# Chunk 1 of a fused attention and feed-forward kernel takes a seven-product gate pair, with its sums on GpSimd

## The chip, the cores and the metric

The kernel runs on one core of a Trainium2 chip. The metric is the device time of one execution in microseconds (us); the time before is 314.78 us, the median of three runs (314.7 to 315.67). The engines are TensorE (PE in the profile, with its weight loads as PEld), VectorE (DVE), ScalarE (ACT), GpSimd (POOL) and SyncE (SP). SP only issues DMAs here. Each engine takes its instructions in the order of the program, and waits at an instruction whose semaphores aren't there yet.

## The reference

Windowed attention over 8 batches of 576 positions and 8 heads of 64 (heads 0 to 3 with a window of 32, heads 4 to 7 with a window of 128 at a dilation of 4), whose output is the input `x` of a gated feed-forward block of 4608 tokens:

```python
scores = scale * np.matmul(q, k.transpose(0, 1, 3, 2))
scores = np.where(masks[None, :, :, :], scores, -1000000000.0)
attn = np.exp(scores - np.max(scores, axis=-1, keepdims=True))
attn = attn / (np.sum(attn, axis=-1, keepdims=True) + 1e-09)
out = np.matmul(attn, v)
x = out.transpose(0, 2, 1, 3).reshape(B * S, H * D)      # 4608 x 512
g = x @ w_gate                                            # 512 x 1536
gelu = 0.5 * g * (1.0 + erf(g * inv_sqrt2))
return (gelu * (x @ w_val) @ w_out)                       # 1536 x 512
```

## The kernel before

The 4608 tokens are nine chunks of 512. Each chunk c has a **gate stage** (x times the gate and value weights, twelve blocks of 128 columns of the inner width, giving `u_all`) and an **output stage** (`u_all` times the output weights). The attention of the next batch is done inside the stages of the chunk: its scores, sums and numerators stand between the output stage's matmuls, because chunk c needs batch c and a part of c - 1 only.

The order is written out by hand. `gate_words(c)` and `out_words(c)` give a string of words, and `run_program` (L1000) walks it and emits each word's instructions on their engines, in that order. A number n takes the next n matmuls of the stage's list. `g` and `u` are the gelu (ACT, L1028) and the product with the value half (DVE, L1033) of a block; `k` the sums of `u_all` for the output stage (DVE); `Kw@p` part p of the sums of the output weights `wo` number w, into `wx` (`weight_sums`, L754, on DVE); `h` the sums of the gate weights of a pair of blocks (`gate_sums`, L645, on GpSimd for pair 1); `Sn@..` the scores of head pair n (batch n // 4); `P`, `M`, `D`, `N`, `l`, `r`, `X` the steps of the softmax, where `X` (DVE, L614) writes x into `xT`.

Most products are done with seven products in place of eight on 2 x 2 blocks. In the output stages of chunks 1 to 8 this is done throughout (`seven`, L812), with the sums `wx` of the weights and `ux` of the data. In the gate stages it is done for some pairs of blocks (word `f`, `ffn1_seven`, L692): pair 1 (blocks 2 and 3) in chunks 2 and 3, two pairs in chunks 4 to 7, three in chunk 8, none in chunk 1. Such a pair is 28 matmuls of 256 columns, where the direct way takes 16 of 512 columns. Its products 1, 2 and 3 read `xT` itself. Products 6, 7, 5 and 4 read four sums of x, the tiles `x_sum` (word `x`, `x_sums`, L674): a chain of four elementwise operations, on GpSimd for the chunks in `free_pool` and on DVE otherwise. The products come in the order 1, 2, 6, 7, 5, 4, 3, spread between the direct blocks by `BLOCKS[c]`: a list of how many products follow each direct half block, and a string of what else is emitted there.

Loading a batch takes three steps. `F b` (`load_first`) has SP issue the loads of q and k of batch b as fp32 into the buffer `stage` (L210, L213, L224), and GpSimd cast them to fp16 into `s16` (L217, L229). `H b` (`load_rest`) has SP issue the transposes of `s16` (L272) and the loads of v (L241, L246, L250), which GpSimd casts too (L254). `R` in gate stage 2 is `H 3`, `F 4` and `H 4` together, and there the v of batch 3 is loaded by DMAs that GpSimd issues (L313, L321, L332). `stage` has three slots, which the loads use again and again. `F3`, the q and k of batch 3, stands at the head of gate stage 1.

Of the kernel before, what the change touches and what calls it, by code (L numbers as in the profile page):

```python
# [21 lines left out]
def kernel(  # L22
# [11 lines left out]
    B, H, S, D = q.shape  # L34
# [3 lines left out]
    NHP = H // 2  # L38
# [5 lines left out]
    NCH = NT // CH  # L44
    NNB = DFF // P
# [128 lines left out]
    def rows_in(src, r):  # L174

        return src.rearrange("h (p r) d -> p h (r d)", r=r)
# [450 lines left out]

    IN_PLACES = {c: {1: (1, 4), 2: (4, 1)} for c in range(4, 7)}
    IN_PLACES[2] = IN_PLACES[3] = {1: (1, 4)}
    IN_PLACES[7] = {1: (1, 4), 2: (2, 3)}  # L630
    IN_PLACES[8] = {1: (1, 2), 2: (6, 3), 3: (4, 5)}
    IN_SEVEN = {c: list(IN_PLACES[c]) for c in IN_PLACES}
    sums_at = {1: 0, 2: CH, 3: 2 * CH}
    free_pool = range(3, NCH)

    def sums_of(j, s):

# [282 lines left out]
    for h in range(0, HK, 2):  # L920
        for t, src, eng in ((0, q, nc.sync), (1, k, nc.scalar)):
            first = eng.dma_start(out=first_p[:, t, h : h + 2], in_=rows_in(src[0, h : h + 2], 6))
# [41 lines left out]
    def gate_banks(c, nb):  # L964

        if c == 0:
            return ((4, 5), (6, 7))[nb] if nb < 2 else ((0, 1), (2, 3))[nb % 2]
        if c in IN_SEVEN:
            if c == NCH - 1:
                return (3, 5) if nb == 10 else (0, 7)  # L970
            if c > 6 and nb > 1:
                return (3, 4) if nb == 11 else (5, 6) if nb % 2 else (0, 7)
            if nb in (1, 11):
                return (1, 4)
            return (4, 1) if nb == 9 and c < 4 else (0, 7)
        return ((0, 7), (1, 6) if c == 1 else (1, 4))[nb % 2]

    SEVEN = range(1, NCH)

    def gate_list(c):  # L980

        if c in firsts:
            first, seen = [], {}
            for word in firsts[c].split():
                nb, gi, kc = (int(x) for x in word)
                i = seen[nb, gi] = seen.get((nb, gi), 0) + 1
                first.append((nb, gi, (kc, i == 1, i == NKC)))
        else:
            first = [(nb, gi, part) for nb in range(2) for gi in range(2) for part in parts_of(range(NKC))]
        order = [(nb, gi) for nb in range(2, NNB) if nb // 2 not in IN_SEVEN.get(c, ()) for gi in range(2)]  # L990
        if c == 0:
            order = [(nb + n, gi) for nb in range(2, 10, 2) for gi in range(2) for n in range(2)] + order[16:]
        rest = [(nb, gi, part) for nb, gi in order for part in parts_of(range(NKC))]
        return [lambda m=m: ffn1_part(c, m[0], m[1], gate_banks(c, m[0])[m[1]], [m[2]]) for m in first + rest]
# [14 lines left out]
    def run_program(c, words, mms, banks):  # L1009
# [3 lines left out]
        for word in words.split():  # L1013
# [12 lines left out]
            elif kind == "g":  # L1026
                g = ffn.tile([P, CH], F16, tag="g")
                nc.scalar.activation(g, ps[:, gate_banks(c, args[0])[0], :], AF.Gelu)  # L1028
                tiles["g", args[0]] = g
            elif kind == "u":  # L1030
# [49 lines left out]
    def gate_words(c):  # L1080

        if c == 0:
            return (
# [4 lines left out]
            )  # L1088
        loads = {1: "F3", 2: "R", 3: "F5 H5", 4: "F6 H6", 5: "F7 H7"}.get(c, "")
        sums = [""] * NNB  # L1090
        if c in SEVEN:
            for j in range(NKP - 1):
                sums[2 * j + 1] += f" k{j}@0" + (f" k{j}@1@2 k{j}@2@2" if j % 2 else "")
        if c == min(SEVEN):
            for n, nb in enumerate((1, 2, 2, 4, 4, 4, 5, 6, 6, 8, 8, 8)):
                sums[nb] += f" K{n // 4}@{n % 4}"
        before = "" if c == NCH - 1 else f"q6@1@{c - 1}"
        last = f" u{NNB - 1} k5@0 k5@1 k5@2" if c > 6 else ""
        first = "7 G 1 g0 2 u0 4 g1 2 u1" if c < NCH - 1 else ""
        if c in IN_SEVEN:  # L1100
            words = seven_words(c)
            loads = f"{loads} x" if c == 2 else f"x z0 z1 {loads}" if c == 3 else f"x z1 {loads}" if c < 6 else "x z1 h3@0 h3@1 h3@2 h3@3" if c < 7 else "x" if c < NCH - 1 else loads
            return f"{before} {loads} {first} {words} 4 g{NNB - 1} {BLOCKS[c][2]} 4 {BLOCKS[c][3]}"
        blocks = [f"4 g{nb} 4 u{nb}{sums[nb]}" for nb in range(2, NNB - 1)]
        if c == 1:
            blocks[8] += f" S{2 * NHP}@12+S{2 * NHP + 1}@14"
        rest = " ".join(blocks)
        if c == 1:
            return f"{loads} 8 G 3 g0 1 u0 3 g1 1 u1{sums[1]} {rest} 4 g{NNB - 1} 4"
        return f"{before} {loads} {first}{sums[1]} {rest} 4 g{NNB - 1} 4{last}"  # L1110

    one = (
        [0, 1, 1, 0, 1, 1, 0, 1, 1, 1, 0, 0, 0, 0, 0],
        "||k0@0||k2@0||||k3@0|k3@1@2|U k3@2@2|U|U k1@0|k4@0 k1@1@2|k1@2@2",
    )
    two = (
        [0, 2, 2, 2, 2, 2, 2, 2, 0, 0, 0],
        "k0@0||||k3@0||k1@0|U|U k4@0 k1@1@2|U k2@0|k4@1@2",
    )
    both = ([0, 2, 2, 2, 2, 2, 2, 2, 0, 0, 0], "k0@0||||k3@0|||U|U k4@0|U k1@0 k2@0|k2@1@3")  # L1120
    BLOCKS = {c: (*two, "", "") for c in range(4, 7)}
    BLOCKS[3] = (*one, "", "")
    early = "h2@0||k0@0 h2@1||k2@0||h2@2||k3@0 h2@3|"
    BLOCKS[2] = (one[0], one[1].replace("||k0@0||k2@0||||k3@0|", early).replace("U k1@0", "U k1@0 S12@12+S13@15"), "", "")
    three = ([0, 3, 3, 3, 3, 3, 3, 3, 0, 0, 0], "||||k0@0|||k1@0|U k4@0|U|U k2@0 k3@0")
# [4 lines left out]
    def seven_words(c):  # L1130

        places = IN_PLACES[c]
        order = (1, 2, 6, 7, 5, 4, 3)
        turns = [(j, product) for j in places for product in order]
        if c > 6:
            turns = [(j, product) for product in order for j in places]
        if len(places) > 2:
            turns = [("_abc".index(w[0]), int(w[1])) for w in in_turn.split()]
        groups = [f"f{j}@{product}@{places[j][order.index(product) % 2]}" for j, product in turns]
        pairs = list(places)  # L1140
        direct = [nb for nb in range(2 if c < NCH - 1 else 0, NNB - 1) if nb // 2 not in pairs]
        slots, after = BLOCKS[c][0], BLOCKS[c][1].split("|")
        words = [groups.pop(0) for _ in range(slots[0])] + [after[0]]
        for n, nb in enumerate(direct):
            for part in range(2):
                words.append(f"4 {'gu'[part]}{nb}")
                for _ in range(slots[2 * n + part + 1]):
                    words.append(groups.pop(0))
                words.append(after[2 * n + part + 1])
        assert not groups  # L1150
        return " ".join(words)

    def out_words(c):

        if c == 0:
            return (
                "h1@0 h1@1 h1@2 h1@3 V1 F2 S6@4+S7@6 1 E P6 11 P7 1 M6 S4@4+S5@6 M7 1 P4 6 P5 M4 2 D6@40+D7@60 l6 l7 M5 r6 r7 6 w2@0 4 w1@0 4 "
                "w0@0 H2 N6@50+N7@20 D4@52+D5@22 X6 l5 X7 l4 r4 r5 10 N4@20+N5@40 X4 X5 2 e3@0"
            )
        if c > 6:  # L1160
            return "12 q0@1 x8 12 q1@1 12 q2@1 12 q3@0 12 q4@0 12 q5@0 12 q6@1" if c < NCH - 1 else "L"
        i, j, k, l = (NHP * (c + 1) + n for n in range(NHP))
        v0 = " v0" if 2 < c < 6 else ""
        some = "k5@1@2 k5@2@2" if len(IN_SEVEN.get(c, ())) < 2 else "k5@1@2@3 k1@2@2 k3@2@2 k5@2@2"
        after = f"S{l + 1}@12+S{l + 2}@15" if 1 < c < 6 else ""
        return (
            f"E P{i} P{j} 1 u11 k5@0 11 q0@0 M{i} M{j}{v0} {some} 12 q1@1 8 "
            f"S{k}@1+S{l}@4 D{i}@11+D{j}@41 P{k} P{l} 8 q2@0 M{k} M{l} 8 l{i} l{j} r{i} r{j} q3@0 "
            f"12 N{i}@10+N{j}@40 D{k}@12+D{l}@42 q4@0 X{i} l{l} X{j} l{k} r{l} r{k} 12 q5@0 {6 if c < 3 else 4} "
            f"N{k}@13+N{l}@43 {after} X{l} X{k} {6 if c < 3 else 8}"  # L1170
        )
# [10 lines left out]
    def run_chunk(c):  # L1182

        banks = out_banks(c)
        run_program(c, gate_words(c), gate_list(c), banks)
        run_program(c, out_words(c), out_list(c, banks), banks)
# [31 lines left out]
```

## Time and profile before

One profiled execution took 314.36 us, with a span of 312.6 us from the first to the last instruction. It is split here by the starts of the stages, as the chain of the work that ended last has them. A row holds the length of the stage and the busy time of each engine, in us.

| stage | from, us | length | PE | DVE | ACT | POOL |
|---|---|---|---|---|---|---|
| output 0 | 41.90 | 13.36 | 13.36 | 8.33 | 8.60 | 8.42 |
| output 1 | 76.55 | 11.98 | 11.98 | 10.59 | 9.48 | 3.37 |
| gate 2 | 88.53 | 20.89 | 20.89 | 17.53 | 11.31 | 10.52 |
| output 3 | 142.56 | 12.26 | 12.26 | 10.91 | 9.42 | 4.61 |
| gate 4 | 154.82 | 20.68 | 20.68 | 16.79 | 14.36 | 12.74 |
| output 4 | 175.50 | 11.76 | 11.66 | 10.37 | 8.75 | 2.10 |

The busy time of PE is read as the time in which any matmul is under way; where it equals the length of a stage, PE never waited there. The mean duration of a matmul in the profile (379 ns for 512 columns) is longer than its share of a stream, because consecutive matmuls overlap.

### The profile page before, as it was taken

To read this page: it belongs to the slowest core of one execution; us is meant where nothing else is said; L and a number is where in the kernel's file an instruction comes from. 1 tells how busy PE (TensorE), PEld (TensorE's weight loads), DVE (VectorE), ACT (ScalarE), POOL (GpSimd) and SP (SyncE) were. 2 spreads that over 40 slices of the span, in tenths; PEclk is the share of its full clock that TensorE was granted. 3 is DMA by queue.
4 is the path that set the end of the run, shared out by engine and by line. 5 is a ranking of instruction groups with operands and counts; after the bars stand their busy time and mean duration, and the time that the engine had idled before them with its cause. 6 is when DMAs were issued, how large, how long until landed. Compare 5 with 4: busy or idle time off the path is not lost.

```text
span 312.6 us, 8913 instructions
## 1 busy us (share of the span) xinstructions
PE 306.2 (98%) x3645; PEld 198.9 (64%) x3645; DVE 238.4 (76%) x425; ACT 189.0 (60%) x320; POOL 126.2 (40%) x174
## 2 busy tenths in 40 slices
PE   7999999999999999999999999999999999999995
PEld 4754555445855486557756685668566856687674
DVE  6773657698897896589868986998698859936972
ACT  2673376534774586547767677777677765427640
POOL 8884774321358073627074327412750073000000
PEclk9999999999999999999999999999999999999999
DMA  8999997897799999789788978995100220021004
GB/s 187 188 200 206 204 202 137 219 235 180 174 282 167 192 192 192 197 197 234 154 238 191 211 183 220 229 182 157 67 3 1 69 69 2 0 94 42 2 0 135
DMA packets 110792, 47.17 MB, mean 151 GB/s; under 512 B 83616, under 2 KB 110240, under 8 KB 110752
## 3 DMA queue, kind: packets, MB, share of 16 engines
q1 hardware_dynamic: 97248, 38.29, 54.9%
q0 software_dynamic: 12944, 7.67, 17.9%
q10 hardware_dynamic: 560, 0.66, 0.8%
q8 instruction: 28, 0.46, 0.6%
q14 instruction: 12, 0.10, 0.1%
HBM read 37.75 MB, written 9.44 MB: 151 GB/s over the span
## 4 chain that ended last, share of the span: by engine, by line
PE 92%; DVE 2%; DMA 2%; ACT 1%; issue 1%; POOL 1%
PE ps L623 44%; PE ps L812 23%; PE ps L692 13%; PE ps L458 7%; PE ps L737 3%; DMA xT<-in_k_dram 2%; PE ps L378 1%; DVE u_all L1033 1%; ACT P L488 1%; DVE xT L614 0%; DVE ux L778 0%; DVE u_all L733 0%; PE ps L447 0%; POOL xT L182 0%; DVE ux L773 0%
## 5 line engine op out<-in xcount | busy, mean ns | idle before, releaser
L623 PE MATMUL ps<-xT,wv 128*128 128x512 f16 x328 | 85.6, 379 | 0.0
L623 PE MATMUL ps<-xT,wg 128*128 128x512 f16 x328 | 84.7, 379 | 0.1
L1028 ACT ACTIVATE g<-ps 128x512 f16<-128x512 f32 x82 | 48.9, 597 | 57.9 <-PE ps L623 57.8
L1033 DVE SCALAR_TENSOR_TENSOR u_all<-g,ps 128x512 f16<-128x512 f16 x82 | 56.0, 684 | 34.8 <-PE ps L623 18.4
L623 PEld LDWEIGHTS <-wg 128*128 128x128 f16 x328 | 31.8, 98 | 33.2 <-issue 0.2
L623 PEld LDWEIGHTS <-wv 128*128 128x128 f16 x328 | 32.1, 98 | 31.7 <-issue 0.8
L812 PEld LDWEIGHTS <-u_all 128*128 128x128 f16 x390 | 36.3, 98 | 7.0 <-issue 0.3
L812 PE MATMUL ps<-wx,ux 128*128 128x256 f16 x288 | 35.2, 272 | 0.1
L812 PE MATMUL ps<-wo,u_all 128*128 128x256 f16 (+1 forms) x294 | 35.2, 271 | 0.0
L217 POOL CAST s<-stage 128x640 f16<-128x640 f32 x24 | 18.8, 812 | 38.5 <-DMA stage<-in_q_dram 24.0
L614 DVE TENSOR_TENSOR xT<-ps,rb 128x576 f16<-128x576 f32 x32 | 29.0, 936 | 4.5 <-PE ps L458 2.9
L488 ACT ACTIVATE P<-ps 128x832 f16<-128x832 f32 (+1 forms) x32 | 25.3, 835 | 11.4 <-PE ps L458 11.3
L812 PEld LDWEIGHTS <-ux 128*128 128x128 f16 x288 | 28.1, 98 | 4.0 <-issue 0.3
L254 POOL CAST v<-stage 128x1152 f16<-128x1152 f32 x11 | 13.1, 1188 | 39.6 <-DMA stage<-in_v_dram 31.3
L692 PEld LDWEIGHTS <-xT 128*128 128x128 f16 x208 | 20.2, 98 | 8.4
L674 POOL TENSOR_TENSOR x_sum<-xT 128x512 f16<-128x512 f16 x12 | 14.0, 1170 | 27.9 <-DVE xT L614 26.5
L733 DVE SCALAR_TENSOR_TENSOR u_all<-g,quarter 128x256 f16<-128x256 f16 x47 | 23.2, 497 | 2.7 <-ACT g L724 2.7
L773 DVE TENSOR_TENSOR ux<-u_all 128x512 f16<-128x512 f16 x48 | 23.4, 493 | 0.8
L585 ACT ACTIVATE lg<-ps 128x576 f32<-128x576 f32 x30 | 18.8, 655 | 7.3 <-PE ps L458 4.3
L724 ACT ACTIVATE g<-quarter 128x256 f16<-128x256 f32 x47 | 19.2, 415 | 4.0 <-DVE quarter L716 3.9
L692 PE MATMUL ps<-x_sum,xT 128*128 128x256 f16 x156 | 21.4, 273 | 0.0
L229 POOL CAST s<-stage 128x512 f16<-128x512 f32 x24 | 17.3, 752 | 6.1 <-DMA stage<-in_q_dram 4.3
(120 smaller groups left out, 432.7 us busy)
## 6 DMA issues: line engine op xcount, KB each, us to landing
out_dram<-part SPq DMA_DIRECT2D x30, 256.0 KB, 3.2
stage<-in_v_dram SPq DMA_DIRECT2D x28, 144.0 KB, 3.6
stage<-in_q_dram SPq DMA_DIRECT2D x24, 128.0 KB, 3.7
stage<-in_k_dram SPq DMA_DIRECT2D x24, 128.0 KB, 2.9
stage<-in_q_dram SPq DMA_DIRECT2D x6, 512.0 KB, 4.6
stage<-in_k_dram SPq DMA_DIRECT2D x6, 512.0 KB, 5.5
stage<-in_v_dram SPq DMA_DIRECT2D x20, 128.0 KB, 2.9
wo<-in_moe_w_out_dram POOLq DMA_DIRECT2D x3, 512.0 KB, 16.6
```

Source lines behind the costliest of these rows:

```text
L217: nc.gpsimd.tensor_copy(s16[:, 1280 * t + 640 * g : 1280 * t + 640 * g + 640].rearrange("p (k c) -> p k c", k=5), st_of(i).rearrange("p (k ...
L458: nc.tensor.matmul(o[cols], lhs[rows], rhs[rows], start=st, stop=end, skip_group_check=True)
L488: nc.scalar.activation(pt[:, 0 : src.shape[1]], src, AF.Exp, bias=0.0, scale=scale)
L614: nc.vector.tensor_tensor(dst, num, rb, ALU.mult)
L623: nc.tensor.matmul(ps[:, bank, :], w[:, kc, ns], xT[kc][:, tok], start=first, stop=end)
L692: nc.tensor.matmul(ps[:, bank, 2 * P * m : 2 * P * m + 2 * P], left[:, k], right[:, k], start=first and m == 0 and k == 0, stop=k == 1, sk ...
L724: nc.scalar.activation(g, t[:, 0 : 2 * P], AF.Gelu)
L733: nc.vector.scalar_tensor_tensor(dst, g, by, t[:, 2 * P : 4 * P], ALU.mult, ALU.mult)
L773: nc.vector.tensor_tensor(ux[:, j, 0:2], k0, u_all[:, 2 * j : 2 * j + 2, hi], ALU.subtract)
L812: lambda o=o, s=s[:, P * p : P * p + P], t=t[:, c0:c1], st=st, end=end: nc.tensor.matmul(o, s, t, start=st, stop=end, skip_group_check=True)
L1028: nc.scalar.activation(g, ps[:, gate_banks(c, args[0])[0], :], AF.Gelu)
L1033: nc.vector.scalar_tensor_tensor(u_all[:, nb, :], tiles.pop(("g", nb)), -USCALE if c in SEVEN and nb % 2 else USCALE, val, ALU.mult, ALU.mult)
```

## The change

Chunk 1 joins the chunks with a seven-product gate pair: pair 1, blocks 2 and 3, in banks 1 and 4. Its x sums go to GpSimd (`free_pool` gets 1), and the word `x` is put behind `F3` at the head of gate stage 1. The twelve parts of the output weights' sums (`K`), all in gate stage 1 before, are split: the eight of `wo` 0 and 1 go to output stage 0, the four of `wo` 2 stay. The scores of batch 2 in gate stage 1 move a bank on and a little forward. The first scores of batches 4 and 5 (`S16`, `S17` and `S20`, `S21`) go from the ends of output stages 2 and 3 into gate stages 3 and 4. The gate weights' sums for pair 1 (`h1`) stay where they were, at the head of output stage 0.

```diff
     IN_PLACES[2] = IN_PLACES[3] = {1: (1, 4)}
+    IN_PLACES[1] = {1: (1, 4)}
...
-    free_pool = range(3, NCH)
+    free_pool = (1, *range(3, NCH))
...
             if nb in (1, 11):
-                return (1, 4)
+                return (1, 6 if c + nb == 2 else 4)
             return (4, 1) if nb == 9 and c < 4 else (0, 7)
-        return ((0, 7), (1, 6) if c == 1 else (1, 4))[nb % 2]
+        return ((0, 7), (1, 4))[nb % 2]
...
-        if c == min(SEVEN):
-            for n, nb in enumerate((1, 2, 2, 4, 4, 4, 5, 6, 6, 8, 8, 8)):
-                sums[nb] += f" K{n // 4}@{n % 4}"
-        before = "" if c == NCH - 1 else f"q6@1@{c - 1}"
+        before = "" if c in (1, NCH - 1) else f"q6@1@{c - 1}"
         last = f" u{NNB - 1} k5@0 k5@1 k5@2" if c > 6 else ""
         first = "7 G 1 g0 2 u0 4 g1 2 u1" if c < NCH - 1 else ""
+        if c == 1:
+            first, loads = "8 G 3 g0 1 u0 3 g1 1 u1", f"{loads} x"
         if c in IN_SEVEN:
             words = seven_words(c)
-            loads = f"{loads} x" if c == 2 else f"x z0 z1 {loads}" if c == 3 else ...
+            loads = loads if c == 1 else f"{loads} x" if c == 2 else f"x z0 z1 {loads}" if c == 3 else ...
             return f"{before} {loads} {first} {words} 4 g{NNB - 1} {BLOCKS[c][2]} 4 {BLOCKS[c][3]}"
         blocks = [f"4 g{nb} 4 u{nb}{sums[nb]}" for nb in range(2, NNB - 1)]
-        if c == 1:
-            blocks[8] += f" S{2 * NHP}@12+S{2 * NHP + 1}@14"
         rest = " ".join(blocks)
-        if c == 1:
-            return f"{loads} 8 G 3 g0 1 u0 3 g1 1 u1{sums[1]} {rest} 4 g{NNB - 1} 4"
...
-    BLOCKS[3] = (*one, "", "")
+    BLOCKS[3] = (one[0], one[1].replace("U k1@0", "U k1@0 S16@12+S17@15"), "", "")
+    BLOCKS[4] = (two[0], two[1].replace("k4@0", "k4@0 S20@12+S21@15"), "", "")
+    BLOCKS[1] = (
+        one[0],
+        one[1].replace("||k0@0||k2@0||||k3@0|", "K2@0||k0@0|K2@1|k2@0|K2@2|||k3@0 K2@3|").replace("k1@2@2", "k1@2@2 S8@12+S9@15"),
+        "",
+        "",
+    )
...
         if c == 0:
             return (
-                "... l6 l7 M5 r6 r7 6 w2@0 4 w1@0 4 "
-                "w0@0 H2 N6@50+N7@20 D4@52+D5@22 X6 l5 X7 l4 r4 r5 10 N4@20+N5@40 X4 X5 2 e3@0"
+                "... l6 l7 M5 K0@0 K0@1 r6 r7 6 w2@0 4 w1@0 4 "
+                "w0@0 H2 N6@50+N7@20 D4@52+D5@22 X6 l5 X7 K0@2 K0@3 l4 r4 r5 10 N4@20+N5@40 X4 X5 K1@0 K1@1 K1@2 K1@3 2 e3@0"
             )
...
-        after = f"S{l + 1}@12+S{l + 2}@15" if 1 < c < 6 else ""
+        after = f"S{l + 1}@12+S{l + 2}@15" if 3 < c < 6 else ""
```

The diff gives `x` one letter; what it does to an engine's queue is seen in the order of its instructions. On GpSimd, from the cast of the v of batch 1 in output stage 0 on, the program before has this (the first four L217 and L229 rows are batch 2, `v_102` is the v of batch 2, the second L217 and L229 rows are `F3`, and `v_100` is the v of batch 3 from `R`):

```order
L254 CAST v_101<-stage 128x1152
L217 CAST s_107<-stage 128x640 x4
L229 CAST s_107<-stage 128x2x4x64 x4
L297 COPY q_104<-q_104 128x8x16
L254 CAST v_102<-stage 128x1152 x2
L217 CAST s_107<-stage 128x640 x4
L229 CAST s_107<-stage 128x2x4x64 x4
L313 DMA v_100<-in_v_dram 64x2x256
```

and the changed program this, from the same v of batch 2 on:

```order
L254 CAST v_102<-stage 128x1152 x2
L217 CAST s_107<-stage 128x640 x4
L229 CAST s_107<-stage 128x2x4x64 x4
L675 TENSOR_TENSOR x_sum<-xT 128x512
L675 TENSOR_TENSOR x_sum<-xT,x_sum 128x512
L675 TENSOR_TENSOR x_sum<-xT 128x512
L675 TENSOR_TENSOR x_sum<-xT,x_sum 128x512
L313 DMA v_100<-in_v_dram 64x2x256
```

The four x sums of chunk 1 stand behind the eight casts of batch 3's q and k, and ahead of the DMAs that load batch 3's v. The order on SP is the same in both programs.

On TensorE, in gate stage 1 after the second half of block 5, the program before goes on with the next direct block:

```order
L623 LDWEIGHTS wv_94
L623 MATMUL ps<-xT,wv_94 128x512
L623 LDWEIGHTS wg_90
L623 MATMUL ps<-xT,wg_90 128x512 [waits Activation_49]
L623 LDWEIGHTS wg_90
```

The changed program has product 6 of the pair there, the third of its seven products (what an instruction waits for stands in brackets):

```order
L623 LDWEIGHTS wv_94
L623 MATMUL ps<-xT,wv_94 128x512
L693 LDWEIGHTS xT [waits Activation_49]
L693 MATMUL ps<-x_sum,xT 128x256 [waits Pool_49]
L693 LDWEIGHTS xT
L693 MATMUL ps<-x_sum,xT 128x256
```

The first matmul of product 6 waits for GpSimd, and all later matmuls of the kernel are behind it on TensorE. (Where block 5's second half stands in the chunk differs between the two, since blocks 2 and 3 are no longer direct.)

On DVE, at the end of output stage 0, the program before stores three output tiles, writes the x of batch 1 and starts on the blocks of gate stage 1:

```order
L493 TENSOR_TENSOR P_994<-P_994,two_p 128x832
L750 TENSOR_SCALAR osb<-ps 128x512 x3
L614 TENSOR_TENSOR xT<-ps,rb 128x576 x4
L1033 SCALAR_TENSOR_TENSOR u_all<-g,ps 128x512 x2
L773 TENSOR_TENSOR ux<-u_all 128x512
```

The changed program has eight of the weight sums among them:

```order
L493 TENSOR_TENSOR P_994<-P_994,two_p 128x832
L761 TENSOR_TENSOR wx_110<-wo_96 128x512
L763 TENSOR_TENSOR wx_110<-wx_110,wo_96 128x512
L751 TENSOR_SCALAR osb<-ps 128x512 x3
L614 TENSOR_TENSOR xT<-ps,rb 128x576 x2
L765 TENSOR_TENSOR wx_110<-wo_96 128x512
L767 SCALAR_TENSOR_TENSOR wx_110<-wx_110,wo_96 128x512
L614 TENSOR_TENSOR xT<-ps,rb 128x576 x2
L761 TENSOR_TENSOR wx_111<-wo_97 128x512
L763 TENSOR_TENSOR wx_111<-wx_111,wo_97 128x512
L765 TENSOR_TENSOR wx_111<-wo_97 128x512
L767 SCALAR_TENSOR_TENSOR wx_111<-wx_111,wo_97 128x512
```

Two sums stand ahead of the stores, two between the pairs of x writes, and four behind the last x write.

More of the change, by code (lines that the diff above doesn't have):

```diff
@@ L1093, in gate_words @@
                 sums[2 * j + 1] += f" k{j}@0" + (f" k{j}@1@2 k{j}@2@2" if j % 2 else "")
-        if c == min(SEVEN):
-            for n, nb in enumerate((1, 2, 2, 4, 4, 4, 5, 6, 6, 8, 8, 8)):
-                sums[nb] += f" K{n // 4}@{n % 4}"
-        before = "" if c == NCH - 1 else f"q6@1@{c - 1}"
+        before = "" if c in (1, NCH - 1) else f"q6@1@{c - 1}"
         last = f" u{NNB - 1} k5@0 k5@1 k5@2" if c > 6 else ""
         first = "7 G 1 g0 2 u0 4 g1 2 u1" if c < NCH - 1 else ""
+        if c == 1:
+            first, loads = "8 G 3 g0 1 u0 3 g1 1 u1", f"{loads} x"
         if c in IN_SEVEN:
             words = seven_words(c)
-            loads = f"{loads} x" if c == 2 else f"x z0 z1 {loads}" if c == 3 else f"x z1 {loads}" if c < 6 else "x z1 h3@0 h3@1 h3@2 h3@3" if c < 7 else "x" if c < NCH - 1 else loads
+            loads = loads if c == 1 else f"{loads} x" if c == 2 else f"x z0 z1 {loads}" if c == 3 else f"x z1 {loads}" if c < 6 else "x z1 h3@0 h3@1 h3@2 h3@3" if c < 7 else "x" if c < NCH - 1 else loads
             return f"{before} {loads} {first} {words} 4 g{NNB - 1} {BLOCKS[c][2]} 4 {BLOCKS[c][3]}"
         blocks = [f"4 g{nb} 4 u{nb}{sums[nb]}" for nb in range(2, NNB - 1)]
-        if c == 1:
-            blocks[8] += f" S{2 * NHP}@12+S{2 * NHP + 1}@14"
         rest = " ".join(blocks)
-        if c == 1:
-            return f"{loads} 8 G 3 g0 1 u0 3 g1 1 u1{sums[1]} {rest} 4 g{NNB - 1} 4"
         return f"{before} {loads} {first}{sums[1]} {rest} 4 g{NNB - 1} 4{last}"
@@ L1156, in out_words @@
             return (
-                "h1@0 h1@1 h1@2 h1@3 V1 F2 S6@4+S7@6 1 E P6 11 P7 1 M6 S4@4+S5@6 M7 1 P4 6 P5 M4 2 D6@40+D7@60 l6 l7 M5 r6 r7 6 w2@0 4 w1@0 4 "
-                "w0@0 H2 N6@50+N7@20 D4@52+D5@22 X6 l5 X7 l4 r4 r5 10 N4@20+N5@40 X4 X5 2 e3@0"
+                "h1@0 h1@1 h1@2 h1@3 V1 F2 S6@4+S7@6 1 E P6 11 P7 1 M6 S4@4+S5@6 M7 1 P4 6 P5 M4 2 D6@40+D7@60 l6 l7 M5 K0@0 K0@1 r6 r7 6 w2@0 4 w1@0 4 "
+                "w0@0 H2 N6@50+N7@20 D4@52+D5@22 X6 l5 X7 K0@2 K0@3 l4 r4 r5 10 N4@20+N5@40 X4 X5 K1@0 K1@1 K1@2 K1@3 2 e3@0"
             )
```

## The prediction, made before the changed kernel ran

> **What bounds the kernel now.** I read the page's first part, then the busy time by stage, then the chain of work that ended last.
>
> ```profile
> span 312.6 us, 8913 instructions
> PE 306.2 (98%) x3645; PEld 198.9 (64%) x3645; DVE 238.4 (76%) x425; ACT 189.0 (60%) x320; POOL 126.2 (40%) x174
> ```
>
> TensorE lacks 6.4 us of the span. The view by stage (length, then the busy time of each engine with its instructions) shows that none of it lies in gate stages 1 and 3:
>
> ```profile
> 55.26:76.55 21.29, 21.29 (x134) 9.80 (x133) 17.39 (x34) 9.26 (x15) 5.63 (x8) 1.00 0.90 211
> 109.42:122.23 12.81, 12.47 (x282) 10.45 (x280) 12.13 (x17) 9.48 (x14) 6.56 (x9) 1.00 1.13 193
> 122.23:142.56 20.33, 20.33 (x111) 10.61 (x109) 13.58 (x27) 11.32 (x21) 9.39 (x10) 1.00 0.79 202
> ```
>
> The first row is gate stage 1, the second output stage 2, which lacks 0.34 us, the third gate stage 3. So time is TensorE's work plus whatever makes TensorE wait, and a wait of TensorE goes into the total one for one. The chain in order of time (start, length, what) gives the work's shape in gate stage 1 and, as a pattern with one seven-product pair, gate stage 3:
>
> ```profile
> 55.26 18.99 PE ps L623 x88
> 74.25 0.47 PE ps L458 x36
> ...
> 76.55 3.49 PE ps L812 x32
> ...
> 122.23 4.32 PE ps L623 x20
> 126.55 0.44 PE ps L692 x4
> 126.98 0.86 PE ps L623 x4
> 127.85 0.44 PE ps L692 x4
> 128.28 1.73 PE ps L623 x8
> 130.01 0.44 PE ps L692 x4
> ```
>
> A direct matmul (L623) takes 4.32 / 20 = 0.216 us of the stream, one of a seven-product pair (L692) 0.44 / 4 = 0.11 us.
>
> **The change, part by part.** *The pair itself.* Sixteen direct matmuls go (16 x 0.216 = 3.46 us), 28 short ones come (28 x 0.109 = 3.05 us): 0.41 us less. Stage against stage it is 0.49: gate stage 3 has what the new gate stage 1 will have but for the scores of batch 2, so 20.33 + 0.47 = 20.80 against 21.29. I take **-0.49 us**.
>
> *The x sums.* Product 6 is the third of the pair, and the first that reads one of them. In gate stage 3 it starts at 130.01 - 122.23 = 7.78 us. Both stages begin with 16 direct matmuls and keep the same slots, so in the new gate stage 1 TensorE comes to it at 55.26 + 7.78 = 63.04 us. When is its sum there? GpSimd runs in order, and the change puts the four sums behind the eight casts of batch 3's q and k. The timeline of GpSimd before shows when these run (start, length; in brackets the idle time ahead and what ended it):
>
> ```profile
> 61.48 2.79 POOL L229 CAST s<-stage 128x512 f16<-128x512 f32 x4 [1.44 <-DMA stage<-in_q_dram]
> 67.62 0.30 POOL L297 COPY q<-q 128x128 f16<-128x128 f16 x1 [3.35 <-DMA q<-s]
> 74.86 1.15 POOL L254 CAST v<-stage 128x1152 f16<-128x1152 f32 x1 [6.95 <-DMA stage<-in_v_dram]
> 78.85 1.22 POOL L254 CAST v<-stage 128x1152 f16<-128x1152 f32 x1 [2.83 <-DMA stage<-in_v_dram]
> 83.22 1.80 POOL L217 CAST s<-stage 128x640 f16<-128x640 f32 x2 [3.16 <-DMA stage<-in_q_dram]
> 88.18 1.39 POOL L217 CAST s<-stage 128x640 f16<-128x640 f32 x2 [3.16 <-DMA stage<-in_k_dram]
> 89.51 1.55 POOL L229 CAST s<-stage 128x512 f16<-128x512 f32 x2
> 92.12 1.18 POOL L229 CAST s<-stage 128x512 f16<-128x512 f32 x2 [1.06 <-DMA stage<-in_k_dram]
> ...
> 123.05 1.15 POOL L674 TENSOR_TENSOR x_sum<-xT 128x512 f16<-128x512 f16 x1 [4.22 <-DVE xT L614]
> 124.28 1.16 POOL L674 TENSOR_TENSOR x_sum<-xT,x_sum 128x512 f16<-128x512 f16 x1
> ```
>
> The first row is batch 2; the casts from 83.22 on are batch 3's, and the last ends at 92.12 + 1.18 = 93.30 us, more than a stage behind the words that emit it. GpSimd isn't busy; it waits for transfers, and their issue is late. The queue of SP:
>
> ```profile
> 76.43 2.38 SPq L210 DMA_DIRECT2D stage<-in_q_dram  x4
> 84.93 0.60 SPq L224 DMA_DIRECT2D stage<-in_q_dram  x1
> 85.63 1.42 SPq L224 DMA_DIRECT2D stage<-in_k_dram  x1
> 87.17 3.38 SPq L835 DMA_DIRECT2D out_dram<-part  x4
> ```
>
> SP comes to batch 3's loads at 76.43 us, after the stores of chunk 0, the transposes of batch 2 and its v, and the order on SP is unchanged. None of those waits for a matmul of gate stage 1, so a stopped TensorE neither hastens nor delays them. Product 6 reads the second sum made. From the start of the first sum to the end of the second it is 124.28 + 1.16 - 123.05 = 2.39 us, so by these rows the sum is there at 93.30 + 2.4 = 95.7 us. It may come sooner: the last load took 6.4 us from its issue to its landing, where the six of its kind took
>
> ```profile
> DMA to landing us min/median/max: 4.0/4.9/6.4
> ```
>
> and the stores of output stage 1, which went out right behind it, won't be there. But the casts ahead of the last two (1.39 + 1.55 us from 88.18) hold GpSimd until 91.1, so at best the last pair starts there, 1.0 us earlier: 94.6 us. I take the middle, 95.1. TensorE then waits 95.1 - 63.04 = **+32.1 us** (31.6 to 32.7). Behind product 6 nothing waits longer: the third sum is wanted one direct half block on and comes one operation (1.16 us) later. Queued behind the waiting matmul is the rest of the kernel. Queued behind the sums on GpSimd are the DMAs of batch 3's v: 93.24 us before, about 98 after, for numerators that move out by the whole stall.
>
> *The restart.* TensorE sits idle for 32 us, and no row shows it doing so inside this kernel. The nearest is the start of the program, where it comes from idle as well:
>
> ```profile
> 1.53 3.84 PE L905 MATMUL ps<-ones 128*32 128x32 f16 x73 [1.53 <-DVE ones L67]
> L905 PE MATMUL ps<-ones 128*128 128x512 f16 x4 | 1.9, 627 | 0.0
> L623 PE MATMUL ps<-xT,wv 128*128 128x512 f16 x328 | 85.6, 379 | 0.0
> ```
>
> The first four matmuls of 512 columns take 1.9 us together, 0.47 each against 0.216 in the stream, and 627 ns each against 379. From its first matmul at 1.53 to the end of those it is some 3.7 us at about half rate, which loses half of that. I take **+1.8 us** for the restart, between 0 (the granted clock is 1.00 in every slice of the page, the first too) and 3.6 (twice as long).
>
> The Trainium skill, "TensorE: Matmul & The Clock Gate", section "What's actually happening", says that TensorE's clock falls to half after an idle window of about 3.4 us, and comes back after about 3.4 us of sustained work. By that the restart would cost half of 3.4, an estimate of 1.7 us, in place of the 1.8 above; and the stall would cost nothing more than itself if the rule did not hold. The slow first matmuls agree with it, the granted clock of this profile does not show it.
>
> *The weight sums.* Twelve parts go from a gate stage in which DVE is busy 17.39 of 21.29 us. Two groups stand for them: three of the four parts take about 0.41 us, the fourth 0.68.
>
> ```profile
> L766 DVE SCALAR_TENSOR_TENSOR wx<-wx,wo 128x512 f16<-128x512 f16 x3 | 2.0, 681 | 0.0
> L760 DVE TENSOR_TENSOR wx<-wo 128x512 f16<-128x512 f16 x3 | 1.2, 412 | 0.0
> 49.37 0.69 DVE L750 TENSOR_SCALAR osb<-ps 128x512 f32<-128x512 f32 x1 [1.14 <-PE ps L737]
> 54.83 1.42 DVE L614 TENSOR_TENSOR xT<-ps,rb 128x576 f16<-128x576 f32 x2 [0.96 <-PE ps L458]
> 58.30 0.69 DVE L1033 SCALAR_TENSOR_TENSOR u_all<-g,ps 128x512 f16<-128x512 f16 x1 [2.04 <-ACT g L1028]
> ```
>
> The last three rows are DVE's in output stage 0, with its idle gaps. The two parts ahead of the stores (0.83 us) fit in the gap of 1.14; the next two (1.09) in 0.96, late by 0.13, while x is wanted by the fifth matmul of gate stage 1, at 55.26 + 0.86, and is there at 55.6 instead of 55.5; the last four (1.92) in 2.04. So **0**. If the cover failed, x would be late by 0.1 to 0.9 us, and that much shorter the stall, whose end GpSimd sets: again 0. The four left in gate stage 1 run in the stall.
>
> *The moved scores.* Their matmuls are the same, 0.47 us out of output stages 2 and 3 and into gate stages 3 and 4: 0 for TensorE. What can go is the 0.34 us in output stage 2; by the timeline it isn't at those scores but ahead of them, so I take **-0.2**, between -0.34 and 0. With 32 us of idle TensorE the later loads also have more time; since TensorE lacks nothing in the gate stages after, that gives nothing back.
>
> **The sum.** -0.49 + 32.1 + 1.8 - 0.2 = +33.2 us. The profiled execution took 314.36 us (1.76 beyond its span), so 347.6; the median is 0.42 above it, so **348.0 us**.
>
> **The rivals.** (1) *The sums are early enough.* If batch 3's casts were done by 60 us, the sums would be there before 63.04, and what is left is -0.49 - 0.2: 314.1, no change by measure. The point that decides is the end of the casts, 93.30 against 60.6. For it speaks only that GpSimd idles much of the stage (5.63 us busy of 21.29); against it stands that these idle times end with transfers issued after 76.43. Chance 0.04. (2) *No restart cost*: TensorE goes on at full rate, 346.2 us. The granted clock of 1.00 speaks for it, the first matmuls against. Chance 0.22. (3) *A second wait* follows, because batch 3's v or batch 4 comes too late behind the sums: some 3 us and more, 351 or above. Against it: SP's next work, the stores of output stage 1, moves out with TensorE, while GpSimd loses under 5 us of 32. Chance 0.06. The forecast, a stall of about 32 us with a slow restart, has 0.68.
>
> **How the numbers follow.** Lowest: 31.6 - 0.49 - 0.34 + 0 gives 314.36 + 30.8 = 345.1. Highest: 32.7 - 0.49 + 0 + 3.6 with the 0.42 to the median gives 350.6. This range holds the forecast and rival 2. About 0.3% (0.9 us) is what a measurement can tell from no change: slower takes the forecast, rivals 2 and 3 (0.96); rival 1 falls within it, with 0.01 for a gain beyond it (0.03 and 0.01).
>
> **What would show it.** TensorE busy until about 63 us, then idle until about 95, its wait put down to GpSimd's `x_sum`; the sums on GpSimd right behind the cast that ends at 92 to 93; the first matmuls after it longer than 379 ns; gate stage 1 some 53 to 55 us long, all later stages as before within 0.5 us. Wrong would be: sums that run before 83 us, an idle time under 30 us, or a later stage that has grown.

## The result, and the profile after

The changed kernel takes 345.63 us, the median of six runs (344.9 to 347.08), against 315.0 us for the kernel before, timed on the same chip (six runs, 314.7 to 316.08). The ratio is 1.0983, with a 95% interval of 1.0962 to 1.1003: 30.6 us longer, and slower. The prediction was 348.0 us, with a range of 345.1 to 350.6. The profiled execution took 344.90 us, the shortest of the six and 0.2 us below that range.

The first lines of the page after, and from its view in 40 slices (8.6 us each) the rows of TensorE's busy time and granted clock:

```profile
span 343.2 us, 8950 instructions
PE 307.9 (90%) x3657; PEld 200.9 (59%) x3657; DVE 237.9 (69%) x430; ACT 191.1 (56%) x326; POOL 128.5 (37%) x178
...
PE   8999999300199999999999999999999999999996
...
PEclk9999999855589999999999999999999999999999
```

TensorE's busy time grew by 1.7 us only, its idle time by 28.9, and a little more than all of that lies in one hole, slices 8 to 11. The clock is granted at half rate in most of the hole, and the slice behind it isn't at full rate either. The busy time by stage after, with gate stage 1 cut at the hole (columns as before: length, PE, PEld, DVE, ACT, POOL, then the granted clock, the DMA share and GB/s):

```profile
55.03:62.87 7.84, 7.84 (x40) 3.81 (x39) 6.83 (x14) 4.75 (x7) 3.48 (x6) 1.00 0.90 262
62.87:92.77 29.90, 0.00 (x0) 0.00 (x0) 1.67 (x4) 0.00 (x0) 10.82 (x16) 0.54 0.76 172
92.77:107.74 14.97, 14.97 (x106) 7.75 (x106) 9.02 (x19) 6.62 (x14) 8.67 (x12) 0.88 0.49 39
107.74:119.55 11.81, 11.81 (x246) 9.90 (x244) 9.86 (x16) 9.47 (x14) 0.00 (x0) 1.00 0.15 48
119.55:140.44 20.89, 20.89 (x146) 10.94 (x145) 17.45 (x39) 11.30 (x21) 4.97 (x7) 1.00 0.98 202
140.44:152.29 11.85, 11.85 (x246) 9.93 (x244) 10.42 (x17) 9.47 (x14) 1.94 (x4) 1.00 0.86 165
```

For 29.90 us neither TensorE nor ACT does anything, and DVE 1.67 us of work. Output stage 1 and gate stage 2 (the fourth and fifth row) are as long as before within 0.2 us, and output stage 2 has lost its wait. What ended the hole is seen on GpSimd; its timeline after, in the same columns as before:

```profile
81.62 1.39 POOL L217 CAST s<-stage 128x640 f16<-128x640 f32 x2 [2.68 <-DMA stage<-in_q_dram]
84.60 1.39 POOL L217 CAST s<-stage 128x640 f16<-128x640 f32 x2 [1.59 <-DMA stage<-in_k_dram]
87.83 1.18 POOL L229 CAST s<-stage 128x512 f16<-128x512 f32 x2 [1.85 <-DMA stage<-in_q_dram]
89.20 1.18 POOL L229 CAST s<-stage 128x512 f16<-128x512 f32 x2 [0.20 <-DMA stage<-in_k_dram]
90.33 1.15 POOL L675 TENSOR_TENSOR x_sum<-xT 128x512 f16<-128x512 f16 x1
91.57 1.15 POOL L675 TENSOR_TENSOR x_sum<-xT,x_sum 128x512 f16<-128x512 f16 x1
```

The sums run right behind batch 3's casts, as fast as in the other chunks. The second one ends at 92.72, and the matmuls of TensorE after it are

```profile
92.77 1.01 PE L693 MATMUL ps<-x_sum,xT 128*128 128x256 f16 x4 [29.90 <-POOL x_sum L675]
93.58 1.91 PE L623 MATMUL ps<-xT,wg 128*128 128x512 f16 x4
95.28 1.06 PE L693 MATMUL ps<-x_sum,xT 128*128 128x256 f16 x4
96.14 1.09 PE L623 MATMUL ps<-xT,wv 128*128 128x512 f16 x4
97.06 1.03 PE L623 MATMUL ps<-xT,wg 128*128 128x512 f16 x4
```

with the four direct matmuls at 93.58 taking 1.91 us, where four of the same shape take 1.03 from 97.06 on. Two questions are left: is it the sums' place in GpSimd's queue, and is the slow restart due to the idling?

### The profile page after: what moved, and what is told of

Its sections match the earlier page's. It is cut to its first block, busy times and chain, and to the rows that moved or that the text cites. A ratio compares the mean times of both kernels' runs of the same rounds, so it can differ in the third digit from the quotient of the medians.

```text
span 343.2 us, 8950 instructions
## 1 busy us (share of the span) xinstructions
PE 307.9 (90%) x3657; PEld 200.9 (59%) x3657; DVE 237.9 (69%) x430; ACT 191.1 (56%) x326; POOL 128.5 (37%) x178
## 4 chain that ended last, share of the span: by engine, by line
PE 87%; SPq 4%; DMA 4%; POOL 1%; ACT 1%; DVE 1%; issue 1%; POOLq 0%
PE ps L623 40%; PE ps L813 22%; PE ps L693 13%; PE ps L458 6%; PE ps L738 3%; DMA q<-s 2%; DMA stage<-in_k_dram 2%; SPq L210 1%; PE ps L906 1%; PE ps L378 1%; SPq L241 1%; SPq L213 1%; SPq L246 1%; POOL x_sum L675 1%; PE ps L375 1%
## 5 line engine op out<-in xcount | busy, mean ns | idle before, releaser
L1034 DVE SCALAR_TENSOR_TENSOR u_all<-g,ps 128x512 f16<-128x512 f16 x80 | 54.7, 685 | 65.0 <-PE ps L623 51.0
L623 PE MATMUL ps<-xT,wg 128*128 128x512 f16 x320 | 83.5, 382 | 0.2
L623 PE MATMUL ps<-xT,wv 128*128 128x512 f16 x320 | 83.7, 379 | 0.0
L1029 ACT ACTIVATE g<-ps 128x512 f16<-128x512 f32 x80 | 47.7, 597 | 57.3 <-PE ps L623 55.4
L693 PE MATMUL ps<-x_sum,xT 128*128 128x256 f16 x168 | 24.1, 279 | 29.9 <-POOL x_sum L675 29.9
L623 PEld LDWEIGHTS <-wv 128*128 128x128 f16 x320 | 31.4, 98 | 30.2 <-issue 1.1
L693 PEld LDWEIGHTS <-xT 128*128 128x128 f16 x224 | 22.2, 99 | 40.0 <-issue 30.7
L707 ACT COPY vdiag<-ps 128x512 f32<-128x512 f32 x22 | 12.8, 582 | 37.0 <-POOL x_sum L675 31.2
L675 POOL TENSOR_TENSOR x_sum<-xT 128x512 f16<-128x512 f16 x14 | 16.4, 1169 | 40.2 <-DVE xT L614 38.8
L217 POOL CAST s<-stage 128x640 f16<-128x640 f32 x24 | 18.1, 781 | 31.7 <-DMA stage<-in_q_dram 16.7
L734 DVE SCALAR_TENSOR_TENSOR u_all<-g,quarter 128x256 f16<-128x256 f16 x51 | 25.4, 502 | 2.8 <-ACT g L725 2.8
L725 ACT ACTIVATE g<-quarter 128x256 f16<-128x256 f32 x51 | 20.8, 414 | 4.0 <-DVE quarter L717 3.9
```

Of the source, the lines that this page charges most:

```text
L623: nc.tensor.matmul(ps[:, bank, :], w[:, kc, ns], xT[kc][:, tok], start=first, stop=end)
L675: (nc.gpsimd if c in free_pool else nc.vector).tensor_tensor(out_, first, other, ALU.subtract)
L693: nc.tensor.matmul(ps[:, bank, 2 * P * m : 2 * P * m + 2 * P], left[:, k], right[:, k], start=first and m == 0 and k == 0, stop=k == 1, sk ...
L725: nc.scalar.activation(g, t[:, 0 : 2 * P], AF.Gelu)
L734: nc.vector.scalar_tensor_tensor(dst, g, by, t[:, 2 * P : 4 * P], ALU.mult, ALU.mult)
L1034: nc.vector.scalar_tensor_tensor(u_all[:, nb, :], tiles.pop(("g", nb)), -USCALE if c in SEVEN and nb % 2 else USCALE, val, ALU.mult, ALU.mult)
```

## The experiments

**The x sums ahead of batch 3's casts, still on GpSimd.**

```diff
-            first, loads = "8 G 3 g0 1 u0 3 g1 1 u1", f"{loads} x"
+            first, loads = "8 G 3 g0 1 u0 3 g1 1 u1", f"x {loads}"
```

> The x sums of chunk 1 stay on GpSimd, but stand ahead of the eight casts of batch 3's q and k, behind the two casts of batch 2's v. Theory 1 (the place in GpSimd's queue sets the stall): the v casts end at 78.94 us in the changed kernel's trace, two sums take 2.4, so product 6 starts at about 81.4 in place of 92.77; TensorE idles 18.5 us in place of 29.9, and one execution takes about 333.6 us. Theory 2 (sums on GpSimd are slow as such, or the pair holds up TensorE for a reason of its own): the idle time stays at 30 us and the execution at 345. Theory 3 (the loads of batch 3 end the stall, wherever the sums stand): also 345.

One execution took 334.7 us, with a span of 333.0. GpSimd's and TensorE's timelines in it:

```profile
78.30 1.15 POOL L254 CAST v<-stage 128x1152 f16<-128x1152 f32 x1 [3.40 <-DMA stage<-in_v_dram]
79.41 1.15 POOL L675 TENSOR_TENSOR x_sum<-xT 128x512 f16<-128x512 f16 x1
80.64 1.15 POOL L675 TENSOR_TENSOR x_sum<-xT,x_sum 128x512 f16<-128x512 f16 x1
...
81.84 1.01 PE L693 MATMUL ps<-x_sum,xT 128*128 128x256 f16 x4 [18.94 <-POOL x_sum L675]
```

The wait is 18.94 us against the 18.5 expected (batch 2's v came 0.5 us later than after the change), the execution 1.1 us over its 333.6. The same sums, on the same engine, at another place in its queue: 11 us less. Neither slow sums nor the pair itself explain that, and batch 3's loads don't end the wait here, since their casts come behind the sums; it ends with batch 2's v.

**The x sums one step further ahead, in front of batch 2's v casts.** The two casts are taken out of `H2` and emitted as `z0 z1` behind `x`.

```diff
-        if b < 4:
+        if b < 4 and b != 2:
...
-            first, loads = "8 G 3 g0 1 u0 3 g1 1 u1", f"{loads} x"
+            first, loads = "8 G 3 g0 1 u0 3 g1 1 u1", f"x z0 z1 {loads}"
```

> The x sums of chunk 1 on GpSimd once more, one step further ahead in its queue: behind the copy of batch 2's q, ahead of the two casts of batch 2's v. Theory 1 (the place in the queue sets the stall): the copy ended at 67.15 to 67.23 us in the runs so far, product 6 began 2.43 us after the start of the sums, so it begins at 69.7 in place of 92.77; TensorE idles 6.8 us, and one execution takes about 322 us if the restart costs its 1.8 us after so short an idle time too, 320 if it doesn't. Theory 2 (something else of the pair or its loads adds a wait): over 324.

One execution took 322.1 us, with a span of 320.4:

```profile
67.44 1.15 POOL L675 TENSOR_TENSOR x_sum<-xT 128x512 f16<-128x512 f16 x1
...
69.86 1.01 PE L693 MATMUL ps<-x_sum,xT 128*128 128x256 f16 x4 [6.85 <-POOL x_sum L675]
70.67 1.91 PE L623 MATMUL ps<-xT,wg 128*128 128x512 f16 x4
72.38 0.69 PE L693 MATMUL ps<-x_sum,xT 128*128 128x256 f16 x4
```

Theory 1 again, to 0.1 us: three places in the queue give waits of 29.90, 18.94 and 6.85 us. The restart is slow after the short wait too, if for a shorter time (product 7 takes 0.69 here, 1.06 above).

**The wait filled with matmuls.** `Y` calls `warm`, which multiplies ones into bank 2, unused there.

```diff
-"b": bias_first}
+"b": bias_first, "Y": warm}
...
-        groups = [f"f{j}@{product}@{places[j][order.index(product) % 2]}" for j, product in turns]
+        groups = [f"{'Y130@2 ' * (c == 1 and product == 6)}f{j}@{product}@{places[j][order.index(product) % 2]}" for j, product in turns]
```

> The changed kernel with 130 matmuls of 512 columns of ones into an unused bank ahead of product 6, which leave the result as it is: 130 x 0.216 = 28.1 us of work in the 29.9 us of waiting. If the slow restart comes from idling: the matmuls after the wait run at full rate (product 6 in 0.44 of the chain, in place of 1.01, the four behind it 0.86 in place of 1.71), the granted clock stays at 1.00, and the execution is 1.8 us shorter, 343.2 us. If the restart is slow for another reason (the first use of the sums, the first loads of weights): the same slow matmuls, and 345 us.

One execution took 343.8 us. TensorE's timeline, and the row of its span and clock:

```profile
63.05 28.22 PE L906 MATMUL ps<-ones 128*128 128x512 f16 x130
92.61 0.60 PE L693 MATMUL ps<-x_sum,xT 128*128 128x256 f16 x4 [1.35 <-POOL x_sum L675]
93.05 1.03 PE L623 MATMUL ps<-xT,wg 128*128 128x512 f16 x4
93.91 0.60 PE L693 MATMUL ps<-x_sum,xT 128*128 128x256 f16 x4
94.35 1.03 PE L623 MATMUL ps<-xT,wv 128*128 128x512 f16 x4
95.21 1.03 PE L623 MATMUL ps<-xT,wg 128*128 128x512 f16 x4
...
core 0: 342.1 us, clock 1.000
```

The same product 6, 0.16 us earlier, now restarts at full rate, and the granted clock never falls. From the start of product 6 to that of the fourth group behind it (16 matmuls on) it takes 95.21 - 92.61 = 2.60 us here and 97.06 - 92.77 = 4.29 after the change: idling costs **1.69 us** on top of the wait. The execution is 1.1 us shorter, not 1.8: this single execution lost the rest again in output stages 2 and 5 (12.02 against 11.85 us, 12.57 against 12.18) and behind its last matmul (0.3).

**The x sums on DVE.**

```diff
-    free_pool = (1, *range(3, NCH))
+    free_pool = range(3, NCH)
```

> The x sums of chunk 1 go to DVE (1 is taken out of free_pool), all else as in the changed kernel. Theory 1: the stall of 29.9 us and the slow restart of 1.8 go, which leaves a span of 343.2 - 31.7 = 311.5. But the sums (2.4 us) now stand on DVE behind four weight sums (1.8 us, from 56.33) and ahead of u0, so u0 ends at about 61.2, while block 4 wants its bank at 59.7: TensorE waits 1.5 us there, span about 313.0, ratio to before 1.00 (0.997 to 1.004). If DVE has the slack after all: 0.9965. Theory 2 (the pair itself holds TensorE up): 330 us or more.

The median is 315.89 us of six, the ratio 1.0036 (1.0021 to 1.0052), at the upper end of what was expected. The wait of 30 us is gone; a small one is left where it was expected, at half its size (DVE and TensorE):

```profile
58.62 0.42 DVE L675 TENSOR_TENSOR x_sum<-xT 128x512 f16<-128x512 f16 x1
...
60.62 1.27 DVE L1034 SCALAR_TENSOR_TENSOR u_all<-g,ps 128x512 f16<-128x512 f16 x2
...
61.34 1.02 PE L623 MATMUL ps<-xT,wv 128*128 128x512 f16 x4 [0.72 <-DVE u_all L1034]
```

The four sums hold DVE for 2.0 us there (58.62 to 60.62). They stand behind four weight sums and ahead of `u0`, which comes too late for block 4's bank.

**The x sums on DVE, and the weight sums earlier.** The same edit of `free_pool`, and in output stage 0:

```diff
-"... P7 1 M6 S4@4+S5@6 M7 1 P4 6 P5 M4 2 D6@40+D7@60 l6 l7 M5 K0@0 K0@1 r6 r7 6 w2@0 ..."
-"... X7 K0@2 K0@3 l4 r4 r5 10 N4@20+N5@40 X4 X5 K1@0 K1@1 K1@2 K1@3 2 e3@0"
+"... P7 1 K0@0 K0@1 M6 S4@4+S5@6 M7 1 P4 6 P5 K0@2 K0@3 M4 2 D6@40+D7@60 l6 l7 M5 K1@0 K1@1 r6 r7 6 w2@0 ..."
+"... X7 K1@2 K1@3 l4 r4 r5 10 N4@20+N5@40 X4 X5 2 e3@0"
```

> As the run with the x sums on DVE, and the eight weight sums of output stage 0 stand earlier there, in DVE's idle gaps ahead of the masks, the stores and the last x writes, so that the x sums are the first thing after x is written. Theory 1: x sums from 56.4 to 58.8, u0 until 59.5, ahead of the 59.7 at which block 4 wants its bank; no wait of TensorE over 0.3 us in gate stage 1, span about 311.5, ratio 0.9965 (0.995 to 0.999). Rival (DVE is too full in gate stage 1 with x sums and four weight sums, 19.8 us by the sum of its parts against 20.8): single waits of 0.3 to 1 us, ratio 1.000 or above.

The median is 314.78 us of eleven, the ratio 0.9998 (0.9987 to 1.0008): no change to the kernel before; the expected 0.9965 lies outside the interval. In gate stage 1 TensorE never waits, and the stage takes 20.91 us from its first matmul (55.06) to that of the next stage (75.97), against 21.30 before. Output stage 1, counted the same way, takes 12.32 us against 11.97 and gives that back. Output stage 2 keeps a wait although the scores have left it. The rows are product 6 and the two waits:

```profile
62.85 0.60 PE L693 MATMUL ps<-x_sum,xT 128*128 128x256 f16 x4
...
87.11 0.58 PE L458 MATMUL ps<-P,v 64*64 64x96 f16 x38 [0.23 <-DVE xT L614]
...
120.40 0.58 PE L458 MATMUL ps<-P,v 64*64 64x96 f16 x38 [0.36 <-DVE xT L614]
```

Twice the numerators of a batch wait for DVE to write x and so to free their bank.

**All but the pair.** The kernel before, with the moved scores and the moved weight sums; in gate stage 1 the four parts of `wo` 2 stay behind the blocks that had them.

```diff
-            for n, nb in enumerate((1, 2, 2, 4, 4, 4, 5, 6, 6, 8, 8, 8)):
-                sums[nb] += f" K{n // 4}@{n % 4}"
+            for n, nb in enumerate((6, 8, 8, 8)):
+                sums[nb] += f" K2@{n}"
```

> The kernel before with the moved weight sums (eight in output stage 0) and the moved scores of batches 4 and 5, but no seven-product pair and no x sums in chunk 1. Theory 1: no stall; the moved scores give back some 0.3 us of output stage 2, the weight sums cost nothing, ratio 0.9985 (0.997 to 1.001). Rival (eight weight sums on DVE in output stage 0 hold up x or the stores, and so TensorE): 1.003 or above.

The median is 315.07 us of twelve, the ratio 1.0006 (0.9987 to 1.0026). No stall and no gain. The weight sums cost nothing by measure, though the interval would let up to 0.26%, 0.8 us, pass. The profiled execution has one wait, of 0.22 us, for x in output stage 1; the kernel before and the run below have none there.

**The moved scores alone.** The kernel before with the changes of `BLOCKS[3]`, `BLOCKS[4]` and `after` from the change.

> The kernel before with nothing but the moved scores of batches 4 and 5. Theory 1: output stage 2 loses its wait of 0.34 us (with the 0.47 us of scores gone into gate stage 3), ratio 0.999 (0.997 to 1.000). Rival (that wait belongs to something else than the scores, and stays): ratio 1.000, and TensorE idle by 0.3 us in output stage 2 as before.

The median is 314.79 us of twelve, the ratio 1.0006 (0.9987 to 1.0024). Output stage 2 keeps a wait, a little smaller and with another name (first row before, second row here):

```profile
117.97 0.54 PE L458 MATMUL ps<-P,ones 64*64 64x32 f16 x16 [0.34 <-issue]
...
120.37 0.58 PE L458 MATMUL ps<-P,v 64*64 64x96 f16 x38 [0.21 <-DVE xT L614]
```

A wait stays though the scores are gone, so by these single executions the rival holds for most of it.

## Why the prediction was right, step by step

The path was right: the sums' place in GpSimd's queue, the wait, the slow restart. The size of the wait was not, and that the total fell into the range is in part luck: the stall lay 1.7 us under its own lower bound, and 345.63 is inside because the low end of the range (345.1) left the restart at nothing. Of the prediction's own signs of being wrong, one came, narrowly: an idle time under 30 us (29.90). Gate stage 1 took 52.71 us, also just short of the 53 to 55 named.

**Where TensorE stops: right.** 63.04 us was forecast, 62.87 measured, with a gate stage that began 0.23 us earlier.

**What it waits for: right.** The order of the instructions and the time at which GpSimd came to them before the change sufficed. The three places in GpSimd's queue show it: the sums begin when what stands ahead of them is done, and product 6 follows 2.4 us after their start in each (90.33 to 92.77, 79.41 to 81.84, 67.44 to 69.86). The rival that the sums are early enough fell by 30 us.

**How long: mis-sized.** The term of the stall was 32.1 us (31.6 to 32.7), measured 29.90. The end of the wait was forecast for 95.1, 94.6 at best, and came at 92.77. The step that failed is the bound "the casts ahead of the last two hold GpSimd until 91.1": it took the casts ahead as fixed, while they moved too. SP after the change (first row its first load of batch 3, last row its last one) came to them at 75.46 in place of 76.43, and to the last at 83.43 in place of 85.63:

```profile
75.46 2.23 SPq L210 DMA_DIRECT2D stage<-in_q_dram  x4
...
83.43 0.45 SPq L224 DMA_DIRECT2D stage<-in_k_dram  x1
```

The casts ended 2.9 us earlier, at 90.38 in place of 93.30. Of that, 1.0 us was there when SP came to the loads, and most of it before TensorE stopped: SP was at batch 2's transposes at 59.02 in place of 59.81. The other 1.9 goes with the wait. From SP's first load of batch 3 to the end of its last cast it takes 14.9 us after the change, 14.7 in the filled run and 14.8 in the run with the wait of 6.85 us; in the five programs without a long wait it takes 16.6 to 17.4. So a long wait of product 6, with all that stands behind it, does hasten the loads, filled with other matmuls or not, and the prediction denied that ("a stopped TensorE neither hastens nor delays them"). How it does so stays open. The first two casts took 1.39 us after the change and in the filled run, with DVE idle, and 1.76 to 2.16 in the programs without a long wait; but they took 1.82 in the run with the wait of 6.85 us, which was as fast, so shorter casts alone don't explain it.

**The restart: right.** +1.8 us was forecast from the first matmuls of the program, 1.69 measured against the filled run (1.89 and 1.30 in the two with shorter waits, by the same count of matmuls: 81.84 to 86.33 and 69.86 to 73.76, less 2.60). The granted clock shows it this time. By the windows of TensorE after the change it was still 1.00 from 62 to 64 us, 0.88 on the mean from 64 to 66, and 0.50 from then until between 96 and 98 (columns: length, busy time of TensorE, granted clock, DMA share, GB/s):

```profile
64.00:66.00 2.00, 0.00 (x0) 0.88 1.43 155
...
94.00:96.00 2.00, 2.00 (x8) 0.50 0.00 0
96.00:98.00 2.00, 2.00 (x11) 0.94 0.67 71
```

With two rates, 1.00 and 0.50, a mean of 0.88 puts the fall 1.52 us into the first row, at 65.5, and 0.94 the rise 0.24 us into the last, at 96.2: 2.7 us after TensorE stopped, and 3.5 after it began again. In the runs with waits of 18.94 and 6.85 us the same working gives a fall after 2.3 and 2.7 us and a rise after 3.9 and 2.7. Half of the 3.5, 3.9 and 2.7 us at half rate is 1.7, 1.9 and 1.3, which are the three costs measured. The rule of the Trainium skill, "TensorE: Matmul & The Clock Gate", section "What's actually happening" (half the clock after about 3.4 us idle, back after about 3.4 us of work), agrees with the rise on the whole, and the fall came sooner than its figure in all three. Rival 2, no restart cost, fell.

**The pair: too optimistic by 0.1.** -0.49 us was forecast. Without the wait, in the run with the sums on DVE and the weight sums early, the stage took 20.9 us against 21.3, so -0.4. As a whole the pair brought nothing measurable in this kernel, even with the sums in time.

**The weight sums: 0 by measure.** Their run without the pair lies within 0.26% of the kernel before, 0.8 us, which is no sharp test of 0. The wait of 0.22 us in its output stage 1 follows the masks there (last section).

**The moved scores: within the bounds, wrong in cause.** -0.2 us was forecast, and output stage 2 did lose its 0.34. But with the scores moved alone a wait of 0.21 stayed, so the scores didn't remove it. The waits go with DVE's masks (L493, `two_p`) in that stage, and those with batch 4's casts on GpSimd. The pair of masks took 1.52, 1.61 and 1.75 us in the three programs that waited there (before, the moved scores alone, the weight sums early), all three with those casts beside the masks. It took 1.08 after the change, where the casts ended at 142.0 and the masks began at 146.44, and 1.11 in the run without the pair; neither waited. (With the x sums on DVE it took 1.50, without a wait.) That the casts are the cause is argued from these times; no run moved the casts alone.

**The sum** by spans: gate stage 1 is 52.71 us long against 21.29, so +31.4. The wait, the restart and the pair make 29.90 + 1.69 - 0.4 = 31.2; the other 0.2 is the overlap of consecutive matmuls, which a wait breaks (without one, product 6 starts at 62.85, before the end of the matmul ahead of it, 61.99 + 1.03). The stages behind gave back 0.6, and what lies ahead of output stage 0 another 0.2, which is the difference of single executions. That leaves the 30.6 of the spans. Of the later stages gate stages 3 and 4 grew by 0.6 us each, from 20.3 to 20.9 and from 20.0 to 20.6 between the first matmuls of the stages, with the 0.47 us of scores put into each. (The table ahead of the prediction has 20.68 for gate stage 4, because the chain there enters output stage 4 late, through DVE.) The second-wait rival did not show: what is queued behind the sums, the DMAs of batch 3's v from 94.88, had the whole stage to spare.

## What to carry to other kernels

Before work moves to an idle engine, read when that engine reaches the place in the program, not how busy it is: an engine that waits for transfers most of the time is idle and late at once, and what stands behind those waits in its queue inherits them. The trace of the kernel before has the time already, in the row of the instruction that will stand ahead. A wait of TensorE that lasts until its clock falls, 2.3 to 2.7 us after it stopped in the three runs with long waits, costs more than itself; the wait of 1.35 us in the filled run didn't.

## What the runs showed of the hardware

GpSimd's casts and DVE's masks can lengthen each other. In the run with the sums on DVE and the weight sums early, and then after the change, the same pair of masks in output stage 1 stands beside a cast and without one (first two rows and last row):

```profile
82.20 2.16 POOL L217 CAST s<-stage 128x640 f16<-128x640 f32 x2 [3.13 <-DMA stage<-in_q_dram]
82.17 1.60 DVE L493 TENSOR_TENSOR P<-P,two_p 128x832 f16<-128x832 f16 x2
```

```profile
113.72 1.08 DVE L493 TENSOR_TENSOR P<-P,two_p 128x832 f16<-128x832 f16 x2
```

Two masks take 1.60 us beside two casts, and 1.08 alone; two casts 2.16 beside the masks, and 1.39 alone. The Trainium skill, "SBUF — State Buffer", section "SBUF: two separate sides", says that DVE operations with two SBUF inputs and GpSimd operations that read SBUF hold a shared pair of ports by turns; the rows agree with a loss on both sides, of 0.5 and 0.8 us, though the four took 2.19 us together (82.17 to 84.36), less than the 2.47 of one after the other.

Which side loses depends on a few tenths of a microsecond. In the kernel before, the same masks start 0.53 us ahead of the casts and keep their 1.08 us:

```profile
82.69 1.08 DVE L493 TENSOR_TENSOR P<-P,two_p 128x832 f16<-128x832 f16 x2
```

Only the casts get longer there (1.80 from 83.22), and so it is with the scores moved alone (0.51 ahead: 1.08 and 1.82). In the three programs whose masks start 0.03, 0.13 and 0.42 us ahead of the casts, the masks take 1.60. These three (weight sums early, x sums on DVE, all but the pair) are also those in which TensorE waited 0.22 to 0.23 us for x in output stage 1.
